# Four small edits at the front of a fused attention and GEGLU kernel: wider warming products, 64x64 transposes, two logarithms and four products reordered

## The chip, the cores and the metric

The kernel runs on one core of one Trainium2 chip. The metric is the device time of one execution in microseconds (us), and the number quoted for a kernel is the median of several executions. The profile is of one execution of its own.

## The reference, cut to what matters

Eight batches of sliding-window attention feed one feed-forward block. Half of the heads of a batch see a plain window of 32 positions, the other half a dilated one.

```python
# q, k, v: (8 batches, 8 heads, 576 positions, 64)
mask_plain = (rel >= 0) & (rel < 32)                          # heads 0-3
mask_dil   = (rel >= 0) & (rel < 128) & (rel % 4 == 0)        # heads 4-7
attn = softmax(where(mask, q @ k.T / 8, -1e9));  y = attn @ v
x = y.transpose(0, 2, 1, 3).reshape(4608, 512)
out = (gelu(x @ w_gate) * (x @ w_val)) @ w_out                # 512 -> 1536 -> 512
```

## The kernel before

**The work and its stages.** The 4608 tokens are cut into nine chunks of 512. For each chunk `run_chunk` emits a gate stage (products with `wg` and `wv`, 96 of 128x512, line 583, the gelu on ACT, line 739, and the product of both on DVE, line 744) and an out stage (48 products with `wo`, line 590, and the stores). A batch has 576 tokens, so chunk c needs the attention of batches c and, for its last tokens, c + 1; the attention of batch c + 1 is emitted between the products of chunk c's out stage. The attention of batch 0 stands ahead of everything, and runs while the weights are loaded.

**Who sets the order.** The order is written by hand. The strings that `gate_words` and `out_words` return are read word by word by `run_program`. A bare number emits so many products of the stage; `S`, `D`, `N` are the scores, row sums and numerators of a head pair n on TensorE (joined by `+` two pairs are interleaved, each in 64x64 tiles: `emit_tiles`, line 418), `P` the exponential on ACT (line 448), `M` the mask on DVE (line 453), `l` and `r` the logarithm of the row sums and the exponential of its negative on ACT (lines 545 and 551), `X` the scaled numerator written into `xT` on DVE (line 574), `t` a transpose with its copy out, `g` and `u` the gelu and the product with it, `e` and `w` stores, `G` and `E` the loads of ACT's function tables, `V` the loads of batch 1. Head pairs 4 to 7 belong to batch 1 (4 and 5 plain, 6 and 7 dilated), and `X4` to `X7` fill batch 1's columns of `xT[0]` to `xT[3]`. The order of the first sixteen gate products of a chunk is in `orders`, as three digits: block of columns, gate or value, and which of the four `xT` tiles.

**PSUM.** `ps` has eight banks of 512 words. `win` places row sums and numerators: the numerator of pair 4 lies in banks 5 and 6, the row sums of pair 6 in banks 6 and 7, the numerator of pair 5 in banks 2 and 3, the row sums of pair 7 in banks 3 and 4, and the numerator of pair 7 in banks 4 and 5, in part over the row sums of pair 7. Where two engines use one bank, the program has a wait between them.

**Warming.** While the first loads are under way TensorE runs `warm(80, 7, 32, 32)` (line 661): 80 products of a 128x32 stationary tile with 32 columns, then three of 512 columns.

**Batch 1's queries and keys.** `second` (line 672), called at the word `V`, issues from the POOL queue in this order: the last quarter of `wg` and `wv`, the plain heads of q and k (line 676, into `six`: 96 partitions, 4 heads, 6 rows of 64 each, cast to f16 on the way), the dilated heads (`load_eights`, line 176), the three parts of `wo` (line 156), and the dilated heads of v (lines 294 and 302). Then it hangs the four loads of batch 1's plain v on SP's queue (`load_v`, line 234) behind the landing of the second part of `wo` (`gated`). POOL casts that v to f16 at the word `V1` (`cast_v`, line 247); the numerators `N4` and `N5` need it. The words `t8`, `t10`, `t9`, `t11` turn the plain q and k: `turn_first` makes 12 transposes for each word, 96 rows to 64 partitions by 96 columns (line 351), and one copy from PSUM of 128x576 (line 329 on ACT, 333 on DVE).

Of the kernel before, what the change touches and what calls it, by code (L numbers as in the profile page):

```python
# [21 lines left out]
def kernel(  # L22
# [73 lines left out]

    u32 = u_all.rearrange("p n c -> p (n c)").bitcast(F32)
    first_p = u32[0:R6, :].rearrange("p (t h c) -> p t h c", t=2, h=HK)
    six = s16[0:R6, 0:3072].rearrange("p (t h r d) -> p t h r d", t=2, h=HK, r=6)
    six0 = s16[0:R6, 0:3072].rearrange("p (t g r h d) -> p t g r h d", t=2, g=2, r=6, h=2)  # L100

    def eight(b):

        tails = [xT[2 * b + t][0:R8, 2 * S : 2 * S + HK * 8 * D] for t in range(2)]
        return [t.rearrange("p (h r d) -> p h r d", h=HK, r=8) for t in tails]
# [59 lines left out]
        if "dma" in gate:  # L165
            tc.add_manual_dep(ins.ins, gate.pop("dma").ins.name, SYNC, reason="order of loads")

    def sixes(src, b):

        return src[b, 0:HK, :, :].rearrange("h (p r) d -> p h (r d)", r=6)  # L170

    def load_eights(b, pairs=((0, HK),)):
        for h0, h1 in pairs:
# [153 lines left out]
    def copy(eng, dst, src):  # L327
        if eng == "act":
            nc.scalar.copy(dst, src)
        elif eng == "pool":  # L330
            nc.gpsimd.tensor_copy(dst, src)
        else:
            nc.vector.tensor_copy(dst, src)
# [7 lines left out]
    def turn_first(n, bank, eng):  # L341

        b, kind, hp, t = n // 8, n % 8 // 4, n % 4 // 2, n % 2
        src, rs, runs = (eight(b)[t], R8, 8) if kind else (six[:, t], R6, 6)
        for r in range(runs):
            at, turned = slice(r * rs, (r + 1) * rs), ident[0:rs, 0:rs]
            if kind == b == 0:
                nc.tensor.transpose(ps16[:, bank, at], six0[:, t, hp, r].rearrange("p h d -> p (h d)"), turned)
                continue
            for x in range(2):  # L350
                nc.tensor.transpose(ps16[64 * x : 64 * x + 64, bank, at], src[:, 2 * hp + x, r, :], turned)
        col = ps16[:, bank, 0:S]
        if kind:
            dst = views(b)[3 if t else 1][:, hp].rearrange("p r (i e) -> p r i e", e=2)
            src = col.rearrange("p (e r i) -> p r i e", e=2, r=4)
        else:
            dst = views(b)[2 if t else 0][:, hp, 0:S].rearrange("p (i r) -> p i r", r=6)
            src = col.rearrange("p (r i) -> p i r", r=6)
        copy(("dve", "act")[eng], dst, src)
        if kind and t:  # L360
            rest = views(b)[2][:, hp, S:640].rearrange("p (i r) -> p i r", r=8)
            copy(("dve", "act")[eng], rest, col.rearrange("p (r i) -> p i r", r=8)[:, 64:R8, :])

    def rows_of(n):
        return slice(n // NHP * S, n // NHP * S + S)
# [262 lines left out]
    def warm(n, bank, rows=P, cols=CH):  # L628

        for _ in range(n):  # L630
            nc.tensor.matmul(ps[0:rows, bank, 0:cols], ones[:, 0:rows], ones[:, 0:cols], start=True, stop=True)
# [13 lines left out]

    for h in range(0, HK, 2):
        for t, src, eng in ((0, q, nc.sync), (1, k, nc.scalar)):
            first = eng.dma_start(out=first_p[:, t, h : h + 2], in_=sixes(src, 0)[:, h : h + 2])  # L648
            if t == 0:
                gate["dma"] = first  # L650
    load_v(0, 0, True)
# [6 lines left out]
    v_cast(0, 1)  # L658
    tiles["two", 0] = views(0)

    warm(80, 7, 32, 32)
    warm(3, 7)
    nc.vector.tensor_reduce(class_of, ident.rearrange("p (i r) -> p r i", r=4), axis=mybir.AxisListType.X, op=ALU.max)
    biases()
# [7 lines left out]
    def second():  # L672

        load_w(3)
        for t, src in ((0, q), (1, k)):
            nc.gpsimd.dma_start(out=six[:, t].rearrange("p h r d -> p h (r d)"), in_=sixes(src, 1))
        load_eights(1)
        wo1 = [load_wo(i) for i in range(3)][1]
        v_cast(1, 0, True)
        v_cast(1, 1)  # L680
        two_masks()
        tiles["two", 1] = views(1)
        gate["dma"] = wo1
        load_v(1, 1, True)
# [34 lines left out]

    def run_program(c, words, mms, banks):  # L720

        units = {"S": two_s, "M": two_m, "D": two_den, "N": two_num, "T": two_t, "B": two_b, "X": two_x, "A": two_a, "l": two_l, "r": two_r, "P": two_p_of, "t": turn_first, "c": cast_six, "W": idle, "b": bias_first}
        joint = {"S": two_s_mms, "D": two_den_mms, "N": two_num_mms}
        for word in words.split():
            kind, args = word[0], [] if "+" in word else [int(x) for x in word[1:].split("@") if x]
            if "+" in word:
                lists = []
                for part in word.split("+"):
                    n, at = (int(x) for x in part[1:].split("@"))
                    lists.append((joint[part[0]](n, at), odd(n)))  # L730
                emit_tiles(*lists)
            elif kind.isdigit():
                for _ in range(int(word)):
                    mms.pop(0)()
            elif kind in units:
                units[kind](*args)
            elif kind == "g":
                g = ffn.tile([P, CH], F16, tag="g")
                nc.scalar.activation(g, ps[:, gate_banks(c, args[0])[0], :], AF.Gelu)  # L739
                tiles["g", args[0]] = g  # L740
            elif kind == "u":
                nb = args[0]
                val = ps[:, gate_banks(c, nb)[1], :]
                nc.vector.scalar_tensor_tensor(u_all[:, nb, :], tiles.pop(("g", nb)), USCALE, val, ALU.mult, ALU.mult)  # L744
            elif kind in "ew":
                at = args[1] if len(args) > 1 else c
                store(at, args[0], out_banks(at)[args[0]], "act" if kind == "e" else "dve")
            elif kind == "L":
                mms.clear()
                last_block(c, 3, banks[3])  # L750
            elif kind == "V":
                (second, second_v)[args[0] if args else 0]()
            elif kind == "F":
                load_first(args[0])
            elif kind == "H":
                load_rest(args[0])
            elif kind == "R":
                load_rest(3)
                load_first(4)
                load_rest(4)  # L760
            elif kind == "E":
                nc.scalar.preload_act_table_set("natural_log_exp_and_others")
            else:
                nc.scalar.preload_act_table_set("gelu_and_others")  # L764
        assert not mms

    def gate_words(c):

        if c == 0:
            return (  # L770
# [4 lines left out]
            )  # L775
        loads = {1: "F3", 2: "R", 3: "F5 H5", 4: "F6 H6", 5: "F7 H7"}.get(c, "")
        rest = " ".join(f"4 g{nb} 4 u{nb}" for nb in range(2, NNB - 1))
        before = f"e3@{c - 1}" if 1 < c < NCH - 1 else ""
        return f"{before} {loads} 8 G {'5 g0 1 u0 1 g1 1 u1' if c == 1 else '2 g0 2 u0 2 g1 2 u1'} {rest} 4 g{NNB - 1} 4" + (f" u{NNB - 1}" if c > 6 else "")

    def out_words(c):

        if c == 0:
            return (
                "V1 F2 S4@4+S5@6 1 E P4 10 P5 1 M4 S6@4+S7@6 M5 1 P6 6 P7 M6 3 D4@40+D5@60 l4 l5 M7 r4 r5 6 w2@0 4 w0@0 4 "
                "w1@0 H2 N4@50+N5@20 D6@52+D7@22 X4 l6 X5 l7 r6 r7 10 N6@20+N7@40 X6 X7 2 e3@0"
            )
        if c > 6:
            return "12 e0 12 e1 12 e2 12 w3" if c < NCH - 1 else "12 e0 12 e1 12 e2 L"
        i, j, k, l = (NHP * (c + 1) + n for n in range(NHP))  # L790
        y, z = (0, 3) if c % 2 else (5, 2)
        return (
            f"1 u11 4 S{i}@{y}+S{j}@{z} E P{i} P{j} M{i} M{j} 7 e0 5 S{k}@{y}+S{l}@{z} D{i}@{y}1+D{j}@{z}1 P{k} P{l} M{k} M{l} "
            f"7 e1 l{i} l{j} r{i} r{j} 10 N{i}@{y}0+N{j}@{z}0 D{k}@{y}2+D{l}@{z}2 X{i} X{j} 2 e2 l{k} l{l} r{k} r{l} "
            f"10 N{k}@20+N{l}@40 X{k} X{l} 2"
        )

    orders = {
# [4 lines left out]
    }  # L803
# [38 lines left out]
```

## Time and profile before

| | us |
|---|---|
| three executions | 330.27, 329.56, 330.44; median 330.27 |
| the profiled execution, its own time | 329.72 |
| its span, first to last instruction | 327.9 |
| TensorE busy in the span | 321.6 (98%) |
| ACT, DVE, POOL busy | 169.2, 138.7, 78.2 |
| granted TensorE clock, mean | 1.0 |
| DMA moved | 47.70 MB, mean 145 GB/s |

The profiled execution took 329.72 us, 1.8 us more than its span. Busy time of TensorE is counted from the start of a product to its modelled end, and products overlap; the distance from start to start is the measure of pace. The chain of waits follows what ended last back to what released it. Times in a timeline count from the start of the span.

### The profile page before, as it was taken

The page shows a single profiled execution, that of the slowest core. Times are in us where ns is not written, and L with a number is a line of the kernel's source. Part 1 is how long each engine was busy: PE and PEld are TensorE (multiplying, and loading weights), DVE is VectorE, ACT ScalarE, POOL GpSimd, SP SyncE. Part 2 cuts the span into 40 slices and gives each one's busy share as a digit, 9 for nine tenths or more (in the row PEclk, how much of TensorE's full clock was granted, in tenths as well). Part 3 has the DMA queues.
Part 4 walks back from the last instruction along what each step waited for, and adds up shares of the span by engine and source line. Part 5 has one row for each costly group of instructions (what it writes and reads, how often), then busy time and mean ns, then how long its engine had stood idle before and what let it go on. Part 6 is the DMA issues. An engine that isn't in the chain of part 4 may idle for free.

```text
span 327.9 us, 7677 instructions
## 1 busy us (share of the span) xinstructions
PE 321.6 (98%) x3177; PEld 157.0 (48%) x3177; DVE 138.7 (42%) x208; ACT 169.2 (52%) x258; POOL 78.2 (24%) x126
## 2 busy tenths in 40 slices
PE   7999999999999999999999999999999999999995
PEld 5844544444544454445444454445444544444443
DVE  6863645443443444343633444344433354204410
ACT  2663466435863576347734783368435853234321
POOL 8883443402411340242224113311000000000000
PEclk9999999999999999999999999999999999999999
DMA  8999997989797896979789747971000100020002
GB/s 189 189 199 204 205 196 144 280 161 205 197 238 171 151 202 166 263 212 186 202 200 243 165 160 185 225 185 66 32 0 28 73 35 0 0 100 29 0 32 98
DMA packets 106915, 47.70 MB, mean 145 GB/s; under 512 B 83584, under 2 KB 102400, under 8 KB 106880
## 3 DMA queue, kind: packets, MB, share of 16 engines
q1 hardware_dynamic: 96352, 39.47, 51.1%
q0 software_dynamic: 9968, 7.08, 14.2%
q10 hardware_dynamic: 560, 0.66, 0.7%
q8 instruction: 25, 0.41, 0.5%
q14 instruction: 10, 0.08, 0.1%
HBM read 37.75 MB, written 9.44 MB: 144 GB/s over the span
## 4 chain that ended last, share of the span: by engine, by line
PE 82%; DMA 13%; SPq 1%; POOL 1%; issue 0%; ACT 0%; DVE 0%; POOLq 0%; ACTq 0%
PE ps L583 51%; PE ps L590 25%; PE ps L418 6%; DMA wo<-in_moe_w_out_dram 5%; DMA stage<-in_v_dram 4%; DMA wv<-in_moe_w_val_dram 3%; DMA u_all<-in_q_dram 2%; SPq L234 1%; PE ps L614 1%; ACT lg L545 0%; POOL v L247 0%; DVE xT L574 0%; POOL wg L153 0%; POOL vdiag L254 0%; SPq L648 0%
## 5 line engine op out<-in xcount | busy, mean ns | idle before, releaser
L744 DVE SCALAR_TENSOR_TENSOR u_all<-g,ps 128x512 f16<-128x512 f16 x108 | 74.0, 687 | 105.4 <-PE ps L583 91.2
L739 ACT ACTIVATE g<-ps 128x512 f16<-128x512 f32 x108 | 64.3, 597 | 104.8 <-PE ps L583 104.8
L583 PE MATMUL ps<-xT,wg 128*128 128x512 f16 x432 | 114.6, 379 | 0.2
L583 PE MATMUL ps<-xT,wv 128*128 128x512 f16 x432 | 114.0, 379 | 0.0
L590 PE MATMUL ps<-wo,u_all 128*128 128x512 f16 x420 | 97.0, 380 | 0.0
L583 PEld LDWEIGHTS <-wv 128*128 128x128 f16 x432 | 42.2, 98 | 51.1 <-issue 0.5
L583 PEld LDWEIGHTS <-wg 128*128 128x128 f16 x432 | 42.1, 98 | 50.8 <-issue 0.3
L590 PEld LDWEIGHTS <-u_all 128*128 128x128 f16 x420 | 38.7, 98 | 44.5 <-issue 0.3
L574 DVE TENSOR_TENSOR xT<-ps,rb 128x576 f16<-128x576 f32 x32 | 28.7, 936 | 27.7 <-PE ps L418 21.5
L448 ACT ACTIVATE P<-ps 128x832 f16<-128x832 f32 (+1 forms) x32 | 25.3, 834 | 15.0 <-PE ps L418 14.9
L247 POOL CAST v<-stage 128x1152 f16<-128x1152 f32 x13 | 15.3, 1179 | 70.0 <-DMA stage<-in_v_dram 70.0
L601 ACT ACTIVATE osb<-ps 128x512 f32<-128x512 f32 x31 | 18.5, 598 | 20.8 <-PE ps L590 20.3
L210 POOL CAST s<-stage 128x640 f16<-128x640 f32 x24 | 16.6, 720 | 40.9 <-DMA stage<-in_q_dram 23.9
L545 ACT ACTIVATE lg<-ps 128x576 f32<-128x576 f32 x30 | 18.2, 650 | 4.9 <-DVE xT L574 3.3
L551 ACT ACTIVATE rb<-lg 128x576 f32<-128x576 f32 x30 | 19.0, 688 | 0.1
L222 POOL CAST s<-stage 128x512 f16<-128x512 f32 x24 | 14.4, 628 | 11.4 <-DMA stage<-in_q_dram 8.0
L453 DVE TENSOR_TENSOR P<-P,two_p 128x832 f16<-128x832 f16 x14 | 9.4, 675 | 13.8 <-ACT P L448 13.8
L453 DVE TENSOR_TENSOR P<-P,two_d 128x768 f16<-128x768 f16 x14 | 8.5, 609 | 12.8 <-ACT P L448 11.9
L764 ACT ACT_TABLE_LOAD x9 | 11.5, 1283 | 0.2
L418 PEld LDWEIGHTS <-q 64*64 64x64 f16 x576 | 7.7, 107 | 6.5 <-issue 5.5
L418 PEld LDWEIGHTS <-v 64*64 64x64 f16 x600 | 7.6, 107 | 6.5 <-issue 4.6
L418 PE MATMUL ps<-q 64*64 64x96 f16 (+2 forms) x576 | 9.9, 203 | 0.1
(66 smaller groups left out, 124.8 us busy)
## 6 DMA issues: line engine op xcount, KB each, us to landing
out_dram<-osb SPq DMA_DIRECT2D x35, 256.0 KB, 2.4
stage<-in_v_dram SPq DMA_DIRECT2D x32, 144.0 KB, 3.6
stage<-in_q_dram SPq DMA_DIRECT2D x24, 128.0 KB, 3.5
stage<-in_k_dram SPq DMA_DIRECT2D x24, 128.0 KB, 3.1
stage<-in_q_dram SPq DMA_DIRECT2D x6, 512.0 KB
stage<-in_k_dram SPq DMA_DIRECT2D x6, 512.0 KB
stage<-in_v_dram SPq DMA_DIRECT2D x24, 128.0 KB, 2.8
wo<-in_moe_w_out_dram POOLq DMA_DIRECT2D x3, 512.0 KB, 15.9
```

Source lines behind the costliest of these rows:

```text
L210: nc.gpsimd.tensor_copy(s16[:, 1280 * t + 640 * g : 1280 * t + 640 * g + 640].rearrange("p (k c) -> p k c", k=5), st_of(i).rearrange("p (k ...
L418: nc.tensor.matmul(o[cols], lhs[rows], rhs[rows], start=st, stop=end, skip_group_check=True)
L448: nc.scalar.activation(pt[:, 0 : src.shape[1]], src, AF.Exp, bias=0.0, scale=scale)
L453: nc.vector.tensor_tensor(pt, pt, mask, ALU.mult)
L545: nc.scalar.activation(lg, psf[:, c0 : c0 + S], AF.Ln)
L551: nc.scalar.activation(rb, tiles.pop(("lg", n)), AF.Exp, scale=-1.0)
L574: nc.vector.tensor_tensor(dst, num, rb, ALU.mult)
L583: nc.tensor.matmul(ps[:, bank, :], w[:, kc, ns], xT[kc][:, tok], start=first, stop=end)
L590: nc.tensor.matmul(ps[:, bank, :], u_all[:, fc, tb * P : (tb + 1) * P], wo_t[fc // 4][:, fc % 4, :], start=(fc == 0), stop=(fc == NNB - 1),)
L601: nc.scalar.activation(osb, ps[:, bank, :], AF.Copy, bias=0.0, scale=1.0 / USCALE)
L739: nc.scalar.activation(g, ps[:, gate_banks(c, args[0])[0], :], AF.Gelu)
L744: nc.vector.scalar_tensor_tensor(u_all[:, nb, :], tiles.pop(("g", nb)), USCALE, val, ALU.mult, ALU.mult)
```

## The change

There are four edits.

1. The warming is 20 products of 128 columns in place of 80 of 32. The stationary tile stays 128x32.
2. Batch 1's plain q and k are loaded as 64 partitions, 4 heads and 9 rows of 64 (`nine`), q on partitions 0 to 63 and k on 64 to 127. The words `y0` and `y1` (`turn_second`) take the place of `t8`, `t10`, `t9`, `t11`: each turns q and k of one pair of heads together, in 36 transposes of 64x64, in the order of the four quadrants of the array, into two banks, and then copies both out, one on DVE and one on ACT. The copies keep their number and size.
3. In the out stage of chunk 0, `l7` comes ahead of `X5` and `l6` after it; it was the other way round. The words `r6 r7` keep their order.
4. In the gate stage of chunk 1 the products 003 and 013 come ahead of 102 and 112, and `g0` is emitted after eleven products, where it was after thirteen.

On TensorE's queue the first edit takes out 120 of the 160 instructions of the warming (a load of the stationary tile and a product each), and the second adds 48. The queues of DVE, POOL and SP keep their instructions in their order, apart from the shape of the two loads; ACT's has `l7` ahead of `l6` and is else as before.

```diff
-    six = s16[0:R6, 0:3072].rearrange("p (t h r d) -> p t h r d", t=2, h=HK, r=6)
+    nine = [s16[64 * t : 64 * t + 64, 0:2304].rearrange("p (h r d) -> p h r d", h=HK, r=9) for t in range(2)]
...
-    def sixes(src, b):
-        return src[b, 0:HK, :, :].rearrange("h (p r) d -> p h (r d)", r=6)
+    def rows_in(src, r):
+        return src.rearrange("h (p r) d -> p h (r d)", r=r)
...
+    def turn_second(hp, *banks):
+
+        for r in range(9):
+            for t in range(2):
+                rows = slice(64 * t, 64 * t + 64)
+                for x in range(2):
+                    o = ps16[64 * x : 64 * x + 64, banks[t], r * 64 : (r + 1) * 64]
+                    nc.tensor.transpose(o, nine[t][:, 2 * hp + x, r, :], ident[rows, rows])
+        for t in range(2):
+            dst = views(1)[2 if t else 0][:, hp, 0:S].rearrange("p (i r) -> p i r", r=9)
+            src = ps16[:, banks[t], 0:S].rearrange("p (r i) -> p i r", r=9)
+            copy(("dve", "act")[(hp + t) % 2], dst, src)
...
-    warm(80, 7, 32, 32)
+    warm(20, 7, 32, 128)
...
-        for t, src in ((0, q), (1, k)):
-            nc.gpsimd.dma_start(out=six[:, t].rearrange("p h r d -> p h (r d)"), in_=sixes(src, 1))
+        for src, t in zip((q, k), nine):
+            nc.gpsimd.dma_start(out=t.rearrange("p h r d -> p h (r d)"), in_=rows_in(src[1, 0:HK], 9))
...
-                "N1@00 X1 X3 G V 15 g0 u0 g1 u1 8 g2 u2 8 g3 u3 8 g4 u4 8 g5 u5 8 g6 u6 8 g7 u7 8 g8 u8 3 t8@4@1 t10@6@0 "
-                "t9@5@1 t11@7@0 5 g9 u9 8 g10 u10 1 t12@4@1 t14@6@0 t13@5@1 t15@7@0 7 g11 u11"
+                "N1@00 X1 X3 G V 15 g0 u0 g1 u1 8 g2 u2 8 g3 u3 8 g4 u4 8 g5 u5 8 g6 u6 8 g7 u7 8 g8 u8 3 y0@4@5 y1@6@7 "
+                "5 g9 u9 8 g10 u10 1 t12@4@1 t14@6@0 t13@5@1 t15@7@0 7 g11 u11"
...
-        return f"{before} {loads} 8 G {'5 g0 1 u0 1 g1 1 u1' if c == 1 else '2 g0 2 u0 2 g1 2 u1'} {rest} 4 g{NNB - 1} 4" + (f" u{NNB - 1}" if c > 6 else "")
+        return f"{before} {loads} 8 G {'3 g0 1 u0 3 g1 1 u1' if c == 1 else '2 g0 2 u0 2 g1 2 u1'} {rest} 4 g{NNB - 1} 4" + (f" u{NNB - 1}" if c > 6 else "")
...
-                "w1@0 H2 N4@50+N5@20 D6@52+D7@22 X4 l6 X5 l7 r6 r7 10 N6@20+N7@40 X6 X7 2 e3@0"
+                "w1@0 H2 N4@50+N5@20 D6@52+D7@22 X4 l7 X5 l6 r6 r7 10 N6@20+N7@40 X6 X7 2 e3@0"
...
-        1: "000 001 010 011 002 012 100 101 110 111 102 112 003 013 103 113",
+        1: "000 001 010 011 002 012 100 101 110 111 003 013 102 112 103 113",
```

More of the change, by code (lines that the diff above doesn't have):

```diff
@@ L343, in turn_first @@
         b, kind, hp, t = n // 8, n % 8 // 4, n % 4 // 2, n % 2
-        src, rs, runs = (eight(b)[t], R8, 8) if kind else (six[:, t], R6, 6)
+        src, rs, runs = (eight(b)[t], R8, 8) if kind else (None, R6, 6)
         for r in range(runs):
             at, turned = slice(r * rs, (r + 1) * rs), ident[0:rs, 0:rs]
-            if kind == b == 0:
+            if not kind:
                 nc.tensor.transpose(ps16[:, bank, at], six0[:, t, hp, r].rearrange("p h d -> p (h d)"), turned)
@@ L647 @@
         for t, src, eng in ((0, q, nc.sync), (1, k, nc.scalar)):
-            first = eng.dma_start(out=first_p[:, t, h : h + 2], in_=sixes(src, 0)[:, h : h + 2])
+            first = eng.dma_start(out=first_p[:, t, h : h + 2], in_=rows_in(src[0, h : h + 2], 6))
             if t == 0:
@@ L720, in run_program @@
     def run_program(c, words, mms, banks):
-        units = {"S": two_s, "M": two_m, "D": two_den, "N": two_num, "T": two_t, "B": two_b, "X": two_x, "A": two_a, "l": two_l, "r": two_r, "P": two_p_of, "t": turn_first, "c": cast_six, "W": idle, "b": bias_first}
+        units = {"S": two_s, "M": two_m, "D": two_den, "N": two_num, "T": two_t, "B": two_b, "X": two_x, "A": two_a, "l": two_l, "r": two_r, "P": two_p_of, "t": turn_first, "y": turn_second, "c": cast_six, "W": idle, "b": bias_first}
         joint = {"S": two_s_mms, "D": two_den_mms, "N": two_num_mms}
```

## The prediction

> **What bounds the kernel now.** I read the chain of waits first, in order of time: it says where TensorE is the bound and where something else is.
>
> ```profile
> 17.88 8.65 DMA wv<-in_moe_w_val_dram
> ...
> 26.81 15.98 DMA wo<-in_moe_w_out_dram
> ...
> 45.43 5.04 DMA stage<-in_v_dram
> ...
> 50.62 1.16 POOL v L247
> 51.78 0.04 issue
> 51.82 1.02 PE ps L418 x63
> 52.84 0.01 issue
> 52.85 0.77 DVE xT L574
> ...
> 53.70 0.62 ACT lg L545
> 54.32 0.37 issue
> 54.69 0.66 ACT lg L545
> 55.35 0.04 issue
> 55.39 0.54 PE ps L418 x32
> 55.93 0.54 PE ps L590 x2
> 56.47 3.51 PE ps L583 x16
> 59.98 0.04 issue
> 60.02 17.43 PE ps L583 x80
> ```
>
> Columns: start, length, what. Up to 51.8 us the chain is transfers, though TensorE is nearly always busy there. Two points are gates: wv's third part lands at 26.53, and batch 1's plain v is cast by 51.78; TensorE starts the waiting work 0.04 later each time (26.57, 51.82). From 60.02 to the end the chain is TensorE without a hole. So time won ahead of 51.82 counts only if that gate moves; time won between 51.82 and 60.02 counts whole.
>
> Next the timeline of TensorE, for starts and counts:
>
> ```profile
> 18.91 0.24 PE L407 MATMUL ps<-P,vdiag 128*128 128x64 f16 x3 [0.65 <-issue]
> ...
> 35.09 1.21 PE L351 MATMUL ps<-ident,s 96*64 96x96 f16 x48
> ...
> 42.14 0.56 PE L418 MATMUL ps<-q 64*64 64x96 f16 x36
> ```
>
> The first line is a hole that no semaphore ends: single records show 0.853 us from one product to the next, where 0.042 is the pace. The page's "q8 instruction" row has 25 packets, 0.41 MB, so 16 KB each; TensorE has 6354 instructions, hence about 256 per packet. The trace has a q8 packet at 16.67 to 17.61, just ahead of this hole's end. I infer a late refill of instructions: 0.81 us.
>
> **What the Trainium skill says.** (1) "TensorE: Matmul & The Clock Gate", Part 1, gives N/1.2 ns per product cold, N/2.4 + 2.5 warm, and a free-running window of about 3.4 us for the switch. Agrees: 512 columns took 427 ns until 7.5 us, where the full clock is granted, and 216 after. (2) "TensorEngine Tiling (Array Packing)", Gotcha 1, keeps tiles on different rows out of one PSUM bank; the change gives q and k a bank each. (3) "PSUM — Partial Sum Buffer", on bank collisions, wants two engines kept apart by bank. Agrees: `l6` starts at 53.70, 0.09 after `X4` ends, though they share only bank 6, not words. (4) "DMA: Bandwidth & Descriptors", SWDGE vs HWDGE vs iDMA: each engine serves its internal queues in turn. So an instruction packet delays one engine's data; of wo's second part 15 of 16 engines landed by 42.15, the last at 42.78.
>
> **The change part by part.**
>
> *Warming.* 80 products 26.7 ns apart are 2.13 us; 20 of 128 columns at 427/4 = 107 ns are 2.13 too. Start (1.53) and end stay, and so should the moment of the clock's switch: 0.
>
> *120 fewer instructions ahead.* Everything up to the transposes moves forward by 120 places, from there by 72. The refill at the hole falls elsewhere: the place that stalled becomes one in the gate products near 31 us, where 256 instructions last 27 us. The refill before it lands in the row sums near 15.2 us; it is asked for near 9.7, and the others early on took 2.8 to 4.1 us to start, 0.9 to 1.3 to land, and up to 1.3 to be used: it is ready between 13.4 and 16.4, so it costs 0 to 1.2. Net at 19 us: -0.81 to +0.4. All of it is covered: if TensorE is early it waits for wv (26.53), if late it has until 51.8. Value 0.
>
> *Transposes.* Before: 48 at one pair per 42.5 ns, 24 x 42.5 = 1.02 us; from the last product ahead (34.785) to the next (36.237) 1.45. After: 72 in 18 groups of four. Groups of four 64-wide tiles in 64x64 follow each other after 28 to 32 ns in the row sums and numerators, so 18 x 30 = 0.54: -0.48. If the four do not overlap: 36 pairs x 29 (the pace of the 72-wide pairs) = 1.04, so 0. Both loads are now needed at the first group, not k's 0.5 later: k's landed at 34.85, 0.24 ahead. The copies: two on ACT, two on DVE as before, of 0.64 and 0.75, ending near 36.8 either way; `g9` needs ACT then. TensorE is 0.48 earlier from 35.8 on, scores, exponentials and masks of batch 1 follow it, and it reaches the gate at 51.09 instead of 51.57. Behind the gate: 0.
>
> *Loads of q and k.* 768 packets of 768 bytes (79 ns) become 512 of 1152. On a line through 60 ns at 512 bytes and 98 at 1024, one is 107.5: 60.7 becomes 55.0 us over 16 engines, -0.36. By bytes, 0: the queue moved 404 KB per 2 us while these loads ran and 407 on average around them. I take -0.05, since bytes rule. These loads stand ahead of wo in POOL's queue, wo's landing releases SP's four v loads, and they release the cast: this is the one edit that can move the gate early.
>
> *The gate otherwise.* SP's and POOL's queues keep their order; their other producers are transfers. A q8 packet started at 39.24 and one at 43.97; 72 places on, they come near 41 and 47. Each holds one engine about 1 us. v's four loads landed by 49.9 on 14 engines, 50.47 on the last. Bound: -0.6 (none on the last engine) to +1.0; value 0.
>
> *Logarithms.* Now `X4` 52.85 to 53.61, `l6` 53.70 to 54.35, `l7` 54.69 to 55.34; TensorE starts `N6` at 54.96 and waits 0.43 for `l7`, whose row sums `N7` overwrites. After: `l7` needs only row sums done at 52.78, so 52.84 to 53.49, beside `X4`. `X5` now waits for it; DVE was not free for `X5` before 53.53 anyway, so at most +0.03, and `N6`'s wait for `X5` has 0.68 to spare. `l6` stays at 53.70, behind `X4`; ACT's 0.37 of issue falls ahead of it, where it waits anyway. So `N6`+`N7` run 54.96 to 55.38 as `N4`+`N5` did (0.41), plus 0.12 to the next product: 55.50, where it was 55.87. **-0.37.** Then `r6` 54.3, `r7` 54.9 to 55.6, `X6` 55.65 to 56.78, `X7` to 57.85.
>
> *Gate products of chunk 1.* The fifth needs `X6`: it would start at 56.80, waits to 56.83 (0.06 before): -0.03. 003 is now eleventh, at 58.13; `X7` is done 0.28 ahead. ACT's store copy ends at 56.7, its table at 58.0, so `g0` runs 58.55 to 59.15, and the 17th product, which overwrites its bank, starts at 59.42 unhindered; before, `g0` ended at 59.97 and held it from 59.82 to 60.02: **-0.20.** `u0` ends 59.87 for a need at 60.28; `g1`, `u1` at 60.0 and 60.73 for 61.15 and 62.0.
>
> Sum: -0.05 - 0.37 - 0.03 - 0.20 = -0.65. Behind 60 us loads and casts for batch 2 on are ready 7.9 us or more ahead of use, so nothing swallows it. The profiled execution took 329.72 around a span of 327.9: its own forecast is 329.07, span 327.25. The median, 0.55 higher, becomes 330.27 - 0.65 = **329.6**. I count 0.3% (1.0 us) as about what a measurement of this kernel can tell from no change.
>
> **The rivals.**
>
> *Lateness that the new slack takes in.* The profiled execution is 0.55 quicker than the median. If the slower ones were late on TensorE's side of the gates (a longer refill at the hole: 0.25 of slack at 51.8 and none at 26.57 hide little), the new slack, 0.81 and then 0.25 + 0.48, takes that in: -0.65 - 0.55 = -1.2, 329.1. For it: refills took 2.8 to 4.1 us to start. Against: a later v would do the same, and no trace of a slower one is there. Chance 0.40; it ends faster by over 0.3% in nine of ten.
>
> *Little is kept.* `X5` behind `l7` or `l6` behind a longer table or semaphore delay holds `N6`, and only the 0.20 stays: 330.1. Against: the slack of 0.68. Chance 0.06.
>
> *An instruction packet delays v.* The packet near 47 us lands amid v's loads (44 to 50.5), on the engine that is last. Gate +1.0, and if the packet near 41 us hits that engine for wo as well, +2.0: net +0.35 to +1.4, 331.0 in the middle. It decides from a last landing of v past 51.1 (50.47 + 0.65). Against: the packet at 39.24 already fell so. Chance 0.09; over 0.3% in most of it.
>
> *The four quadrants do not overlap.* TensorE reaches the gate at 51.57 as before: no change of the end. It lies within the first case.
>
> **How the numbers follow.** The first case has 0.45, 329.2 to 330.0 by the gate's ordinary scatter; it is within 0.3% but for a tail of 0.05. Faster: 0.05 + 0.36 = 0.41; slower 0.08; same 0.51. The range 328.7 to 330.4 leaves out the far end of each side.
>
> **What would show it.** Right: no hole near 18 us; the transposes in about 0.75 us; TensorE idle 0.5 or more ahead of `N4`, ended by POOL's cast near 51.8; `l7` ahead of `X5`; `N6`+`N7` without a hole; the 17th gate product 7.6 after `N4` (8.2 before). Wrong: a v cast ending a us away from 51.8, a hole near 15 us that reaches past 26.5, or a new one behind 60.

## The result, and the profile after

Sixteen executions of each kernel gave 330.35 us before (329.32 to 330.69) and 329.39 after (328.39 to 330.09), in the median. The ratio is 0.9974, with a 95% interval of 0.9965 to 0.9983. On 330.35 that is -0.86 us, between -1.16 and -0.56 (the two medians lie 0.96 apart). The forecast of -0.65 lies inside, and so does 329.39 in its range.

The execution that was traced for the profile after is the slowest of the sixteen (330.09, span 328.4), and its chain of waits shows why. Columns: start, length, what.

```profile
12.82 0.87 ACT P L461
15.33 1.53 issue
16.86 1.70 PE ps L420 x20
18.55 1.48 PE ps L431 x25
...
20.96 15.97 PE ps L596 x74
36.93 0.78 PE ps L371 x72
...
53.16 0.88 PE ps L431 x63
54.03 2.27 PE ps L603 x10
56.30 0.48 PE ps L431 x40
56.77 0.54 PE ps L603 x2
57.31 20.80 PE ps L596 x96
```

Lines moved by 13 behind the new function: L583 became L596, L590 L603, L418 L431, L545 L558 (one more in `a_turn2`); the `b_` kernels without edit 2 keep the old ones. The hole near 18 us is gone, and one of 1.53 us stands at 15.33, at instruction 446 of TensorE. From there to the end the chain is TensorE; neither wv nor v's cast is in it. What followed on the hole is in the windows of the same kernel (stretch, sum, busy time of PE, PEld, DVE, ACT and POOL, granted clock, DMA share, GB/s):

```profile
15.00:17.00 2.00, 0.47 (x9) 0.33 (x6) 1.19 (x3) 0.81 (x1) 0.79 (x2) 1.00 1.45 192
17.00:18.00 1.00, 1.00 (x16) 0.91 (x15) 0.05 (x1) 0.72 (x2) 1.00 (x3) 0.51 1.45 196
...
19.00:20.00 1.00, 1.00 (x35) 0.98 (x30) 0.54 (x1) 0.95 (x3) 1.00 (x2) 0.50 1.32 171
...
21.00:25.00 4.00, 4.00 (x20) 1.86 (x19) 2.57 (x4) 1.34 (x3) 2.24 (x4) 1.00 1.24 204
```

The clock fell to half from 17.03 to 20.44. So TensorE reached `N4` at 53.09, 0.84 after POOL's cast had ended (52.25), and this execution tells nothing of the usual gate. The stretch behind `N4` can still be read: at 57.31 the chain reaches the gate products of chunk 1, and all 96 run on in 20.80 us without a hole. Before, 16 of them took 3.51 and the next 80 started at 60.02.

A second trace of the changed kernel (`a_again`, 329.54, span 327.8) shows the ordinary course, again in the chain:

```profile
45.15 5.99 DMA stage<-in_v_dram
...
51.29 1.16 POOL v L247
52.45 0.04 issue
52.49 0.94 PE ps L431 x63
53.44 2.26 PE ps L603 x10
55.70 0.48 PE ps L431 x40
56.18 0.54 PE ps L603 x2
56.72 20.82 PE ps L596 x96
```

and in the timeline of TensorE:

```profile
35.14 0.85 PE L371 MATMUL ps<-ident,s 64*64 64x64 f16 x72
...
52.49 0.58 PE L431 MATMUL ps<-P,v 64*64 64x96 f16 x40 [1.05 <-POOL v L247]
```

Here v's cast is back in the chain as the gate, and TensorE stands idle for 1.05 us ahead of `N4` until POOL's cast ends. wv is no gate in this trace: its third part lands at 26.25, and TensorE comes to it at 26.63 without a gap. From 4.68 us to the end of the work the full clock was granted, and no distance over 0.14 us stands at instruction 446.

### The profile page after: what moved, and what is told of

Same layout as the page of the kernel before. It is cut to its first block, busy times and chain, and to the rows that moved or that the text cites. A ratio compares the mean times of both kernels' runs of the same rounds, so it can differ in the third digit from the quotient of the medians.

```text
span 328.4 us, 7604 instructions
## 1 busy us (share of the span) xinstructions
PE 321.4 (98%) x3141; PEld 157.2 (48%) x3141; DVE 139.5 (42%) x208; ACT 169.8 (52%) x258; POOL 78.3 (24%) x126
## 4 chain that ended last, share of the span: by engine, by line
PE 96%; DVE 1%; issue 1%; ACT 0%; POOL 0%
PE ps L596 57%; PE ps L603 29%; PE ps L431 7%; PE ps L420 1%; PE ps L351 1%; PE ps L627 1%; PE ps L348 0%; PE ps L650 0%; DVE vdiag L195 0%; ACT P L461 0%; PE ps L371 0%; DVE q L333 0%; POOL band L117 0%; DVE s L333 0%; DVE ones L67 0%
## 5 line engine op out<-in xcount | busy, mean ns | idle before, releaser
L596 PE MATMUL ps<-xT,wg 128*128 128x512 f16 x432 | 114.8, 380 | 0.0
L596 PE MATMUL ps<-xT,wv 128*128 128x512 f16 x432 | 114.0, 379 | 0.0
L603 PE MATMUL ps<-wo,u_all 128*128 128x512 f16 x420 | 97.0, 380 | 0.0
L596 PEld LDWEIGHTS <-wv 128*128 128x128 f16 x432 | 42.3, 98 | 51.0 <-issue 0.2
L596 PEld LDWEIGHTS <-wg 128*128 128x128 f16 x432 | 42.1, 98 | 50.4
L603 PEld LDWEIGHTS <-u_all 128*128 128x128 f16 x420 | 38.7, 98 | 44.5 <-issue 0.3
L558 ACT ACTIVATE lg<-ps 128x576 f32<-128x576 f32 x30 | 18.3, 651 | 5.0 <-issue 1.8
L466 DVE TENSOR_TENSOR P<-P,two_d 128x768 f16<-128x768 f16 x14 | 9.1, 652 | 13.0 <-ACT P L461 12.2
L431 PEld LDWEIGHTS <-q 64*64 64x64 f16 x576 | 7.7, 107 | 6.7 <-issue 5.5
L431 PEld LDWEIGHTS <-v 64*64 64x64 f16 x600 | 8.0, 111 | 6.0 <-issue 5.5
L431 PE MATMUL ps<-q 64*64 64x96 f16 (+2 forms) x576 | 9.9, 203 | 0.3 <-DVE q L333 0.3
```

Source lines behind the costliest of these rows:

```text
L431: nc.tensor.matmul(o[cols], lhs[rows], rhs[rows], start=st, stop=end, skip_group_check=True)
L466: nc.vector.tensor_tensor(pt, pt, mask, ALU.mult)
L558: nc.scalar.activation(lg, psf[:, c0 : c0 + S], AF.Ln)
L596: nc.tensor.matmul(ps[:, bank, :], w[:, kc, ns], xT[kc][:, tok], start=first, stop=end)
L603: nc.tensor.matmul(ps[:, bank, :], u_all[:, fc, tb * P : (tb + 1) * P], wo_t[fc // 4][:, fc % 4, :], start=(fc == 0), stop=(fc == NNB - 1),)
```

## The experiments

The theory was the prediction's: time ahead of the v cast is hidden, time between `N4` and the 17th gate product of chunk 1 counts whole. The main rival was that slack on TensorE takes in lateness. Times are given as ratios to the kernel before on the same chip. This table gathers them. Its third column is from single records of each trace, so it rests on one execution of each kernel: from the first product of `N4` to the 17th gate product of chunk 1.

| kernel | ratio (95% interval) | `N4` to 17th product, us | `N4` at |
|---|---|---|---|
| before | 1 | 8.20 | 51.82 |
| changed, first and second trace | 0.9974 (0.9965 to 0.9983), 0.9973 (0.9963 to 0.9984) | 7.59, 7.61 | 53.09, 52.49 |
| `b_warm` | 0.9998 (0.9986 to 1.001) | 8.19 | 52.47 |
| `b_order` | 0.9972 (0.9962 to 0.9982) | 7.58 | 52.77 |
| `b_turn` | 0.9979 (0.9971 to 0.9988) | 7.87 | 52.29 |
| `b_act1` | 0.9990 (0.9978 to 1.0002) | 7.88 | 51.91 |
| `a_nologs` | 0.9972 (0.9963 to 0.9981) | 7.68 | 52.28 |
| `a_nogate` | 0.9981 (0.9972 to 0.9990) | 7.82 | 52.29 |
| `a_wo0` | 0.9975 (0.9967 to 0.9983) | 7.61 | 51.86 |
| `a_turn2` | 0.9991 (0.9982 to 0.9999) | 7.58 | 52.30 |
| `a_split` | 0.9965 (0.9951 to 0.9978) | 8.25, 0.66 of it a wait inside `N4` | 51.09 |
| `a_split_wo0` | 0.9972 (0.9961 to 0.9982) | 7.59 | 52.08 |
| `a_w60` | 0.9985 (0.9976 to 0.9994) | 7.59 | 52.40 |

### One edit at a time, and the changed kernel again

**`b_warm`: the kernel before with edit 1 alone.**

```diff
-    warm(80, 7, 32, 32)
+    warm(20, 7, 32, 128)
```

> The kernel before with only the warming products changed. Theory (gates: what is won or lost ahead of the v cast near 51.8 us doesn't count while TensorE is in time for it): 0 in the median, within 0.3 of the kernel before; the instruction refill falls 120 places earlier in the work, so the hole near 18 us is gone and one stands near 15.1 us, of 0.5 to 1.8 us; if it is above some 1.5 us and the clock falls behind it, that execution is late at the v gate (N4 after 52.5). Rival (the refill is what the gain comes from): -0.4 or more. Rival (the hole near 15 us is usually long): +0.5 or more.

Measured: ratio 0.9998, -0.07 us on 330.08. The hole near 18 is gone; at instruction 446, at 15.24, two products stand 0.25 apart, so the hole of 0.5 to 1.8 that was expected there is not in this trace. Edit 1 alone is worth nothing that shows.

**`b_order`: edits 3 and 4 alone.**

```diff
-                "w1@0 H2 N4@50+N5@20 D6@52+D7@22 X4 l6 X5 l7 r6 r7 10 N6@20+N7@40 X6 X7 2 e3@0"
+                "w1@0 H2 N4@50+N5@20 D6@52+D7@22 X4 l7 X5 l6 r6 r7 10 N6@20+N7@40 X6 X7 2 e3@0"
...
-        1: "000 001 010 011 002 012 100 101 110 111 102 112 003 013 103 113",
+        1: "000 001 010 011 002 012 100 101 110 111 003 013 102 112 103 113",
...
-        return f"{before} {loads} 8 G {'5 g0 1 u0 1 g1 1 u1' if c == 1 else '2 g0 2 u0 2 g1 2 u1'} {rest} 4 g{NNB - 1} 4" + (f" u{NNB - 1}" if c > 6 else "")
+        return f"{before} {loads} 8 G {'3 g0 1 u0 3 g1 1 u1' if c == 1 else '2 g0 2 u0 2 g1 2 u1'} {rest} 4 g{NNB - 1} 4" + (f" u{NNB - 1}" if c > 6 else "")
```

> The kernel before with only the order of the two logarithms and of gate stage 1's first products changed. Theory (gates): this is nearly all of the gain, -0.60 (0.37 of it the wait of N6 for l7, 0.20 the wait of the 17th gate product for g0, 0.03 the wait for X6); the 17th gate product starts 7.6 us after N4 instead of 8.2, and the hole near 18 us stays. Rival (the gain comes from lateness that slack takes in): -0.3 or less, in the median of the runs, though the stretch in the trace is the same.

Measured: ratio 0.9972, -0.92 us; the stretch is 7.58, 0.62 shorter than before, as forecast. Alone, these two edits give all that the four give together. The hole near 18 us, expected to stay, is not in this trace: two products stand 0.04 apart at its place. On ACT the hole between the logarithms is still there:

```profile
53.85 0.65 ACT L545 ACTIVATE lg<-ps 128x576 f32<-128x576 f32 x1 [2.76 <-issue]
54.98 0.65 ACT L545 ACTIVATE lg<-ps 128x576 f32<-128x576 f32 x1 [0.47 <-DVE xT L574]
```

ScalarE's wait for `X4` was over at 54.60, and the second logarithm, now `l6`, started 0.37 later. But `N7` needs only the first, and TensorE does not wait.

**`b_turn`: edit 2 alone.**

```diff
-                "N1@00 X1 X3 G V 15 g0 u0 g1 u1 8 g2 u2 8 g3 u3 8 g4 u4 8 g5 u5 8 g6 u6 8 g7 u7 8 g8 u8 3 t8@4@1 t10@6@0 "
-                "t9@5@1 t11@7@0 5 g9 u9 8 g10 u10 1 t12@4@1 t14@6@0 t13@5@1 t15@7@0 7 g11 u11"
+                "N1@00 X1 X3 G V 15 g0 u0 g1 u1 8 g2 u2 8 g3 u3 8 g4 u4 8 g5 u5 8 g6 u6 8 g7 u7 8 g8 u8 3 y0@4@5 y1@6@7 "
+                "5 g9 u9 8 g10 u10 1 t12@4@1 t14@6@0 t13@5@1 t15@7@0 7 g11 u11"
```

`turn_second` and the loads into `nine` are as in the change.

> The kernel before with only batch 1's plain q and k loaded in runs of nine and turned in four 64x64 tiles. Theory (gates): 0 to -0.1; the transposes take about 0.78 us instead of 1.21, and TensorE then waits that much longer ahead of N4, which starts near 51.8. Rival (slack counts in many executions): -0.3 to -0.5.

Measured: ratio 0.9979, -0.69 us (-0.96 to -0.40). The theory's 0 to -0.1 fell. But the rival's slack is not what shows either. In the chain of `b_turn`

```profile
51.09 1.16 POOL v L247
...
52.29 0.94 PE ps L431 x63
53.23 2.27 PE ps L603 x10
55.49 0.58 PE ps L431 x34
56.07 0.54 PE ps L603 x2
56.61 3.51 PE ps L596 x16
60.12 0.04 issue
60.16 17.43 PE ps L596 x80
```

the cast still holds `N4`, and the gain stands behind it: 55.49, where the chain before had ACT's two logarithms with 0.37 us of issue between them and a wait ahead of `N7`, has `N6` and `N7` close together. Edit 2 does not touch the logarithms. What it does to ScalarE's stream is to put one semaphore wait more into it, ahead of one of the copies (137 records of waits and issues in the trace, where the kernel before has 136), so that everything behind stands one place later. The description of the change, which left ACT's queue as it was but for `l7` and `l6`, missed that. Of the 0.69 the stretch holds 0.33 (8.20 to 7.87); where the rest is was not found. `b_order`, which changes nothing ahead of `N4`, is 0.30 beyond its stretch too, so the rest need not be slack, though slack is not excluded.

**`a_again`: the changed kernel as it is.**

> The changed kernel as it is, for another traced execution. The one traced first was the slowest of 16 (330.09), with a hole of 1.53 us near 15.3 and half the clock for 3.4 us behind it. Theory (gates, and that execution an outlier): time of 329.4 in the median, -0.6 to -1.0 against before; a hole near 15.1 that is shorter, full clock behind it, TensorE idle ahead of N4 for 0.3 or more, N4 near 51.8. Rival (the hole of 1.5 us and the clock drop are the rule): the trace shows them again, and N4 stands after 52.5.

Measured: ratio 0.9973, 329.13; the trace is the second one above. `N4` came at 52.49 rather than near 51.8, and TensorE's idle time ahead of it was 1.05.

### Where edit 2's gain comes from

**`b_act1`: the kernel before with one more instruction early on ScalarE.**

```diff
+    nc.scalar.preload_act_table_set("gelu_and_others")
     nc.scalar.preload_act_table_set("natural_log_exp_and_others")
```

> The kernel before with one more instruction at the start of ScalarE's stream (a second table load, for another function set, near 1 us, where ScalarE has nothing to do until 6 us), nothing else. Theory (ScalarE's 0.37 us of issue ahead of l7 is a refill of its instructions that belongs to a place in its stream, instruction 64; one instruction more puts the place on the semaphore wait ahead of l7, which ScalarE reaches while l6 still runs): the hole between l6 and l7 is gone, N6+N7 run without a hole, the 17th gate product starts 7.87 us after N4 instead of 8.20, and the time falls by 0.33. Rival (the hole comes from the wait for X5 or from PSUM that X4 and l6 share): no change, 0.37 of issue is still there.

Measured: ratio 0.9990, -0.33 us (-0.73 to 0.07), and a stretch of 7.88. The interval alone does not exclude 0; the trace shows what changed. The timeline of ACT, the kernel before first:

```profile
53.70 0.65 ACT L545 ACTIVATE lg<-ps 128x576 f32<-128x576 f32 x1 [2.69 <-DVE xT L574]
54.69 0.65 ACT L545 ACTIVATE lg<-ps 128x576 f32<-128x576 f32 x1 [0.34 <-issue]
55.24 1.25 ACT L551 ACTIVATE rb<-lg 128x576 f32<-128x576 f32 x2
```

and then `b_act1`:

```profile
53.79 1.31 ACT L545 ACTIVATE lg<-ps 128x576 f32<-128x576 f32 x2 [2.55 <-DVE xT L574]
55.00 1.25 ACT L551 ACTIVATE rb<-lg 128x576 f32<-128x576 f32 x2
```

The 0.34 of issue is gone with one instruction that has nothing to do with the logarithms. So the hole belongs to a place in ScalarE's stream. Counted from 0 in the built program it is place 64 (63 among the records of the trace): the logarithm `l7` itself before, and in `b_act1` and `b_turn` the semaphore wait ahead of `l7`, which ScalarE meets while `l6` still runs. The other traces agree: a logarithm stands at this place in three kernels (before, `b_warm`, `b_order`), and each starts 0.35 to 0.37 us after what stands ahead of it in the stream; in the other eleven a wait stands there, and none has the hole. That the hole is a fetch of instructions is inferred from this and from TensorE's holes; no DMA record was matched to it.

**`a_nologs`: the changed kernel without edit 3.**

```diff
-                "w1@0 H2 N4@50+N5@20 D6@52+D7@22 X4 l7 X5 l6 r6 r7 10 N6@20+N7@40 X6 X7 2 e3@0"
+                "w1@0 H2 N4@50+N5@20 D6@52+D7@22 X4 l6 X5 l7 r6 r7 10 N6@20+N7@40 X6 X7 2 e3@0"
```

> The changed kernel with the old order of the logarithms (l6 ahead of l7). Theory (the turned tiles already put one more instruction on ScalarE ahead of the logarithms, which takes the refill hole away, so the new order of the logarithms has little left to win): +0.10 against the changed kernel, the 17th gate product 7.7 us after N4. Rival (the prediction's account, the new order is worth 0.37 by itself): +0.37, a wait of 0.4 ahead of N7, the 17th product near 7.97.

Measured: ratio 0.9972, and a stretch of 7.68 against 7.60. `N6` and `N7` run on without the wait of 0.4 ahead of `N7`:

```profile
55.42 0.65 PE L431 MATMUL ps<-P,v 64*64 64x96 f16 x40
```

The new order is worth 0.08 there, not 0.37; in the times it doesn't show.

**`a_nogate`: the changed kernel without edit 4.**

```diff
-        1: "000 001 010 011 002 012 100 101 110 111 003 013 102 112 103 113",
+        1: "000 001 010 011 002 012 100 101 110 111 102 112 003 013 103 113",
...
-        return f"{before} {loads} 8 G {'3 g0 1 u0 3 g1 1 u1' if c == 1 else '2 g0 2 u0 2 g1 2 u1'} {rest} 4 g{NNB - 1} 4" + (f" u{NNB - 1}" if c > 6 else "")
+        return f"{before} {loads} 8 G {'5 g0 1 u0 1 g1 1 u1' if c == 1 else '2 g0 2 u0 2 g1 2 u1'} {rest} 4 g{NNB - 1} 4" + (f" u{NNB - 1}" if c > 6 else "")
```

> The changed kernel with the old order of gate stage 1's first products. Theory: +0.20 against the changed kernel, and a wait of 0.42 ahead of the 17th gate product for g0 is back, which starts 7.80 us after N4. Rival (g0 is in time anyway now that X6 and X7 come 0.37 earlier): 0, the 17th product at 7.60.

Measured: ratio 0.9981, and a stretch of 7.82, +0.22. The chain has the step ahead of the 17th product again:

```profile
56.52 3.56 PE ps L596 x16
60.07 0.04 issue
60.11 17.43 PE ps L596 x80
```

Single records show 0.417 us between the 16th and the 17th product, where 0.216 is the pace, as in the kernel before. The ratio lies 0.0007 to 0.0008 (0.25 us) above the changed kernel's: the size forecast, though the intervals overlap.

### The gate itself

**`a_wo0`: v's loads released by wo's first part.**

```diff
-        wo1 = [load_wo(i) for i in range(3)][1]
+        wo1 = [load_wo(i) for i in range(3)][0]
```

> The changed kernel with SP's four loads of batch 1's plain v released by the landing of wo's first part instead of its second, nothing else. Theory (the v cast is the gate, and TensorE waits 1.3 us ahead of N4 in most executions): the loads and the cast come about 2 us earlier, TensorE reaches N4 near 51.1 without a wait, and the time falls by 0.8 to 1.2 against the changed kernel (328.1 to 328.5). Rival (the transfers share one rate: what v gains, wo's second and third part and the loads behind lose, so TensorE waits at the out products from 44 us on instead): a gain under 0.4, or a loss, with a wait for wo in the trace.

Measured: ratio 0.9975, no gain on the changed kernel. The chain:

```profile
39.69 0.59 SPq L234
...
41.70 8.81 DMA stage<-in_v_dram
...
50.66 1.16 POOL v L247
...
51.86 0.94 PE ps L431 x63
```

SP issued the loads 3.5 us earlier than in `a_again` (39.69 against 43.15), and the last landing moved from 51.14 to 50.51: the transfer took 8.81 where it took 5.99. A landing at 50.51 lies within the scatter of the traces with the old release (50.21 to 51.42), so even those 0.63 are not sure. The rival's first half fits: from 40 to 46 us the DMA moved 194 to 208 GB/s here and 188 to 207 in `a_again`, so what v gained in time it lost in rate. There was no wait for wo.

**`a_split`: the cast of v in two halves.**

```diff
-        cast_v(views(1)[4], 1)
+        src = st_of(1)[:, 0:1152].rearrange("p (e d) -> p e d", d=D)
+        for e in (slice(0, NB2), slice(NB2, 2 * NB2)):
+            nc.gpsimd.tensor_copy(views(1)[4][:, e], src[:, e])
```

> The changed kernel with the POOL cast of batch 1's plain v in two halves, each waiting for its own two of the four loads, nothing else. Theory (the cast, 1.16 us behind the last landing, is what N4 waits for): only half of it, about 0.6, is left behind the last landing; N4 starts 0.55 earlier, at 51.5 to 51.8, and the time falls by 0.5 against the changed kernel. Rival (TensorE is as late as the cast in most executions): no change.

Measured: ratio 0.9965 over five executions of it, median 328.84, the best of all kernels here. Its interval takes in the changed kernel's ratio, so the step from one to the other (-0.3) is not settled by the times. The chain:

```profile
44.79 6.12 DMA stage<-in_v_dram
...
51.03 0.68 POOL v L702
...
51.75 0.94 PE ps L431 x49
```

Behind the last landing (50.91) stands half a cast, 0.68 instead of 1.16. The rest of `N4` and `N5` starts at 51.75, 0.74 ahead of `a_again`'s `N4`, with a landing 0.23 earlier: about 0.5 is the split's, as forecast. The first products of `N4`, which need only the first half, had started at 51.09.

**`a_split_wo0`: both, the split cast and the earlier release.**

```diff
-        wo1 = [load_wo(i) for i in range(3)][1]
+        wo1 = [load_wo(i) for i in range(3)][0]
...
-        cast_v(views(1)[4], 1)
+        src = st_of(1)[:, 0:1152].rearrange("p (e d) -> p e d", d=D)
+        for e in (slice(0, NB2), slice(NB2, 2 * NB2)):
+            nc.gpsimd.tensor_copy(views(1)[4][:, e], src[:, e])
```

> The changed kernel with the cast in two halves and the four loads of v released by wo's first part. Theory (cast as above; v's transfers, released 2.5 us earlier, land only 0.4 us earlier since they share the rate): N4 near 51.2, close to TensorE's own arrival at 51.1; the time 0.8 to 0.9 below the changed kernel's, near 328.4. Rival (wo's third part, delayed by v's packets, holds the out products near 49): a gain of 0.4 or less with a wait for wo.

Measured: ratio 0.9972; the forecast missed. In this trace v's last packet landed at 51.06, no earlier than with the old release, and TensorE was late by itself. Its chain:

```profile
15.89 0.94 issue
...
19.79 16.13 PE ps L596 x74
35.92 0.78 PE ps L371 x72
...
52.15 0.87 PE ps L431 x63
```

The hole at instruction 446 is 0.94 here, and TensorE, without another wait, reached `N4` at 52.08; by single records the cast had ended at 51.86. With the cast ended earlier, TensorE's holes ahead of it begin to count.

**`a_turn2`: each of the 72 transposes twice.**

```diff
-                    nc.tensor.transpose(o, nine[t][:, 2 * hp + x, r, :], ident[rows, rows])
+                    for _ in range(2):
+                        nc.tensor.transpose(o, nine[t][:, 2 * hp + x, r, :], ident[rows, rows])
```

> The changed kernel with each of batch 1's 72 plain transposes issued twice in a row. Theory (TensorE's time ahead of the v cast is free): the group takes about 1.5 us instead of 0.78, TensorE reaches N4 near 51.8 instead of 51.1 and still waits there for the cast; the time stays as the changed kernel's, within 0.25. Rival (TensorE's time ahead of N4 counts): +0.7.

Measured: ratio 0.9991, -0.30 us, where the changed kernel has -0.87: 0.57 lost, between the theory's limit and the rival's 0.7. The timeline of TensorE shows how much cover there was:

```profile
35.40 1.53 PE L372 MATMUL ps<-ident,s 64*64 64x64 f16 x144
...
52.30 0.58 PE L432 MATMUL ps<-P,v 64*64 64x96 f16 x40
```

The cast ended at 52.10 and TensorE came at 52.30. So the 0.68 more was just over the cover in this execution, by 0.2; the 0.57 of the times is larger, but loose, since the intervals of the two kernels almost meet. An execution with a long hole near 15 us has less cover; that such executions make up the rest is not shown. What the traces bear out is that time ahead of the gate is free for as long as TensorE stands idle at `N4`: 0.4 to 1.3 us in the eight traces behind this result in which the whole cast held it, but only 0.07 in the profiled execution before.

### The place of TensorE's hole

**`a_w60`: 60 warming products of 43 columns.**

```diff
-    warm(20, 7, 32, 128)
+    warm(60, 7, 32, 43)
```

> The changed kernel with 60 warming products of 43 columns for 20 of 128, which are as long (about 2.1 us) and put 80 more instructions ahead of everything. Theory (TensorE's instructions come in blocks of 256, and one that is asked for on entering the block before takes 5 to 7 us in this stretch): the place is now near 13.4 us, reached 5.0 us after the one before it at 8.4, so a hole of 0.3 to 2 us stands there and none near 15 or 18; the time stays as the changed kernel's, within 0.3, if the hole is under about 1.5 us and the clock stays full. Rival (the holes belong to the work at 15 and 18 us and not to the count): no hole near 13.4.

Measured: ratio 0.9985, 0.4 us slower than the changed kernel in the median, at the edge of what the intervals tell apart. Its stretch and its `N4` are as usual; its one trace has 0.25 more behind the 17th product, in a stall near 219 us, and whether that is usual for it is not known. The hole is where the count puts it, in the timeline of TensorE:

```profile
13.01 0.36 PE L431 MATMUL ps<-q 64*64 64x96 f16 x8
13.68 0.36 PE L431 MATMUL ps<-q 64*64 64x80 f16 x10 [0.32 <-issue]
```

It parts one group of scores in two, at the same count of instructions (446) at which the kernels with 20 products of 128 columns have theirs in the row sums near 15 us. With 80 products the place is 702, in the diagonal products near 18 (three of four traces have a hole there; `b_order` has none).

## Why the prediction was right, and where its steps were not

**The sum.** -0.65 forecast, -0.86 (-1.16 to -0.56) measured. The part behind `N4` was forecast at -0.60: 8.2 became 7.59 and 7.61. The step from 8.20 to 7.6 is the gain that the traces tie to an edit. What the median has beyond it lies within the interval and is not tied to one: from the 17th to the last product the profiled execution before took 264.35 us, the two of the changed kernel 264.08 and 264.09, and the other eleven traces 264.07 to 264.33, by short stalls near 124, 161 and 219 us that some executions have and others not.

**The logarithms, -0.37: right in size, wrong in cause.** The prediction said that "ACT's 0.37 of issue falls ahead of it, where it waits anyway". In `b_order` it falls behind that wait and delays `l6`, which starts 2.21 after `N4` where 1.88 was forecast; it costs nothing only because TensorE does not need `l6`. In the changed kernel there is no such hole at all (`l6` at 54.37 in `a_again`, 1.88 after `N4`), since edit 2 has moved ScalarE's stream by one place. The step that failed is the costing of edit 2: it counted the copies on ACT and not the wait in front of one of them. Read from the table: the place alone 8.20 to 7.88, then the gate order and the logarithms' order 7.88 to 7.60 (0.19 to 0.22 and 0.05 to 0.08). Two edits take the same 0.33 off TensorE's path, so each looks as if it were its owner: `b_turn` -0.69 and `b_order` -0.92 don't add up to the -0.87 of all four. That the sum came out right with edit 2 priced at nothing behind the gate is luck: its 0.33 happened to be counted already, under edit 3.

**The gate products, -0.20: right.** `a_nogate` puts 0.22 back into the stretch, with the wait of the 17th product.

**The transposes.** The four quadrants do overlap: groups of four follow each other after 32 ns. From the last product ahead to the next one behind it is 1.10 us, where it was 1.45: -0.35, not -0.48. The step ahead of the group (0.31) and the one behind it (0.14) are as before; but from the first transpose to the last there are 0.64, where the forecast put 0.54 for the whole group, since the first step from one group of four to the next takes 0.05 and the last 0.09. It is gained ahead of the gate and hidden there, as forecast, so far as the traces show.

**Warming, 0: right**, by `b_warm` (-0.46 to 0.33). Where the hole near 18 was gone and none stood near 15, TensorE waited for wv, as forecast: 0.4 to 0.6 us near 26.6 in five of the six traces with 20 warming products and no long hole. The hole at the new place was bounded at 0 to 1.2. In the nine traces with 20 the distance at instruction 446 was 0.04 to 0.35 in six, and 1.09, 1.15 and 1.74 in three: one is over the bound, and that half the clock can follow was not foreseen.

**The gate at 51.8: an early execution, taken as the rule.** In the seven further traces with the old release in which the whole cast held `N4`, it started between 52.28 and 52.77. In the other three with the whole cast and the old release (the first trace of the change, `a_turn2`, `b_act1`) TensorE came after the cast, which had ended at 52.25, 52.10 and 51.51. So a late v is the likelier source of the difference between the profiled execution and the median, and not lateness on TensorE's side, where the first rival put it; but the kernel before was traced once, and both kinds of lateness occur. The profiled time less its `N4` hardly differs between the two traces of the change: 277.90 before, 277.00 and 277.05 after. With these the two medians put `N4` near 52.4 in both kernels, by estimate, so the gate hardly moved. The slack of 0.25 that the prediction gave TensorE at 51.8 was 0.14: where nothing holds it, `N4` starts 0.31 after the product ahead (the same three traces), and before it started 0.45 after. The -0.05 for fewer packets stays open: v's last packet landed between 50.80 and 51.14 in the eight traces with turned tiles and the old release, and between 50.21 and 51.42 in the four without.

**The rival of a slower end** (an instruction packet delays v past 51.1) did not come: the median fell, and landings past 51.1 occur with either warming (51.12 in `b_warm`, 51.42 in `b_order`). Whether an instruction packet delayed any of them was not looked at.

## What to carry to other kernels

A hole that the profile puts down to "issue" can belong to a place in an engine's stream rather than to the work at that place: try one instruction more ahead of it before giving a reordering the credit. Before calling a time hidden, measure how deep the cover is and in how many executions; here it was 0.07 to 1.3 us, and 0.68 more in one group used it up. Here a stretch between two nearby events agreed between two executions of one kernel within 0.02 us (7.59 and 7.61), while the landing of v scattered by 1.2 over the traces with the old release.

## What the runs showed of the hardware that was not expected

- TensorE's stream can stall at fixed counts, 256 apart (446 and 702). In the seven traces with a distance over 0.5 us there, the first product came 1.3 to 1.7 us after a 16 KB packet of the instruction queue had landed. That the packet is what TensorE waited for is inferred.
- That packet started at 12.2 to 12.7 in six traces with 20 warming products and at 13.8 to 14.1 in the three with a long hole; nothing lay between. With 80 it started at 16.6 to 16.7 in the three with a hole, and at 15.6 in `b_order`, which has none. What decides it was not found.
- One hole of 1.53 us on TensorE was followed, 1.7 us after it began, by half the clock for 3.41 us; holes of 0.88 to 0.95 in other traces, and an idle time of 1.34 ahead of `N4` in `a_w60`, left the clock full. In all fourteen traces each stretch of full clock is a whole multiple of 3.413 us long (3, 90, 94 or 95 of them), so the clock seems to change only on such a grid. The hole of 1.53 lay within one step of it, 13.62 to 17.03.
- ScalarE's stream lost about 0.35 us at its place 64 where a logarithm stood there (three traces), and nothing with one instruction more ahead of it.
